# A decode kernel's GELU mixer moved from VectorE to GpSimd, with its output weights on a hardware queue in transfers of 120 and 8 partitions

## The chip, the cores and the metric

The kernel runs on one core of one Trainium2 chip. The metric is the device time in microseconds. The kernel before takes 1303.7 us (median of 4 runs, 1302.6 to 1304.4).

Engine names: PE is TensorE, DVE is VectorE, ACT is ScalarE, POOL is GpSimd, SP is SyncE. SP here only issues DMA transfers.

## The reference

One token attends to a cache of 65536 positions, with 8 KV heads of 256 (2 query heads each). Beside it runs a small mixer on the same token: a layer norm, then a sum over 1792 hidden units of GELU, for each of 448 channels. A sigmoid gate blends both.

```python
g = sigmoid((x * gate_w).sum(-1))                  # x: (1, 1, 448)
q = (x @ wq).reshape(16 heads, 256)
p = softmax(q @ k.T / 16)                          # k, v: 8 heads x 65536 x 256, bf16
a = (p @ v).reshape(4096) @ wo                     # wo: 4096 x 448
u = gelu(layernorm(x)[d] * w1[f] + b1[f])          # 448 x 1792
b = u @ w2 + b2
out = g * a + (1 - g) * b
```

K and V are 537 MB together. The output weights `wo` are only 3.67 MB, and the mixer is 14 blocks of 128 hidden units.

## The kernel before

K and V stream in chunks of 8192 positions (4 MB each) through a ring of five 32 KB slots per partition, all on SP's queue. Each chunk is worked on in four steps: transposes on PE, a copy from PSUM on DVE, scores on PE, exp on ACT, a transpose of p on DVE, and P-V on PE four steps later. The output weights of KV head g (512 rows, 448 KB) come on GpSimd's queue, two heads ahead. These are the parts that the change and the argument touch:

```python
def load_wo(g):                                   # GpSimd's (software) queue, 128 partitions
    nc.gpsimd.dma_start(
        out=wo_t[g % 2][:],
        in_=A_wo[g * 512:(g + 1) * 512, :].rearrange("(q p) n -> p q n", p=128),
    )
# ...
def mixer_open(b):
    nc.scalar.activation(out=t_b, in_=h_bc, func=ACT.Square, scale=w1T[:, b], bias=b1T[:, b])
    nc.vector.tensor_scalar(out=u_b, in0=h_bc, ...)            # u = h*w1 + b1
def mixer_mid(b):
    nc.vector.tensor_scalar(out=t_b, in0=t_b, ...)             # C1*u^2 + 1
    nc.vector.tensor_tensor(out=t_b, in0=t_b, in1=u_b, op=ALU.mult)
    nc.scalar.activation(out=t_b, in_=t_b, func=ACT.Tanh, scale=GELU_C0)
def mixer_close(b):
    nc.vector.scalar_tensor_tensor(out=gel, in0=t_b, scalar=1.0, in1=u_b, ...)
    nc.tensor.matmul(y_ps, lhsT=w2T[:, b:b + 1], rhs=gel, ...)
# ... one block every two steps, so the mixer is over after 30 of the 256 steps
for n in range(n_steps + LAG):
    transposes(n, 0); scores(n - 1); transposes(n, 1); p_transpose(n - 1)
    mixer(n)
    epilogue(n)
    p_v(n - LAG)
    # a load of the ring slot that has just come free, on SP
```

The softmax here doesn't subtract the row's maximum and nothing guards it: scores larger than these inputs give would overflow.

Of the kernel before, what the change touches and what calls it, by code (L numbers as in the profile page):

```python
# [8 lines left out]
FP32 = mybir.dt.float32  # L9
# [7 lines left out]
DH = 256  # L17


NB = 64  # L20
# [14 lines left out]
def kernel(  # L35
# [46 lines left out]
    LAST_K = [SB] * STEPS  # L82
    LAST_V = [2 * SB, SB, SB // 2 + 2, SB // 2 - 2]

    def load(item):
        i, is_v = divmod(item, 2)
        g, c = divmod(i, n_chunks)
        src = (A_v_cache if is_v else A_k_cache)[0, g, c * CHUNK:(c + 1) * CHUNK, :]
        src = src.rearrange("(p j) d -> p (j d)", j=NB)
        dst = ring[item % RING]  # L90
        parts = [NB]
        if i == total - 1:
            parts = LAST_V if is_v else LAST_K
        j = 0
        for n in parts:
            nc.sync.dma_start(out=dst[:, j * DH:(j + n) * DH], in_=src[:, j * DH:(j + n) * DH])
            j += n
# [8 lines left out]
    for hh in range(2):  # L106
        nc.sync.dma_start(
            out=wqb[64 * hh:64 * hh + 64, :], in_=A_wq[DA:D, 8 * DH * hh:8 * DH * (hh + 1)]
        )
# [4 lines left out]
    xa = const.tile([128, KA], BF16)  # L114
    xb = const.tile([128, 2], BF16)
    gwa = const.tile([128, KA], BF16)
    gwb = const.tile([128, 1], BF16)
    nc.vector.memset(xb[:], 0.0)
    nc.vector.memset(gwb[:], 0.0)
    x_row = A_x[0, 0]  # L120
    nc.scalar.dma_start(out=xa[:], in_=x_row[0:DA].rearrange("(p k) -> p k", k=KA))
    for hh in range(2):
        nc.scalar.dma_start(
            out=xb[64 * hh:64 * hh + 64, hh:hh + 1], in_=x_row[DA:D].rearrange("(p o) -> p o", o=1)
        )
    nc.gpsimd.dma_start(out=gwa[:], in_=gate_w[0:DA].rearrange("(p k) -> p k", k=KA))
    nc.gpsimd.dma_start(out=gwb[0:64, :], in_=gate_w[DA:D].rearrange("(p o) -> p o", o=1))

    xB = work.tile([128, D], FP32, name="xB")
    nc.gpsimd.dma_start(out=xB[:], in_=x_row.partition_broadcast(128))  # L130
# [11 lines left out]
    def load_wo(g):  # L142
        nc.gpsimd.dma_start(
            out=wo_t[g % 2][:],
            in_=A_wo[g * 512:(g + 1) * 512, :].rearrange("(q p) n -> p q n", p=128),
        )
# [4 lines left out]
    ones_f = const.tile([128, 128], FP32)  # L151
    nc.gpsimd.memset(ones_f[:], 1.0)


    sel = const.tile([128, 2, 2], FP32)
    same = const.tile([128, 4, 32], FP32)
    nc.gpsimd.memset(sel[:], 0.0)
    nc.gpsimd.memset(same[:], 0.0)
    for a in range(4):
        nc.gpsimd.affine_select(  # L160
            out=sel[:].rearrange("p h r -> p (h r)"), in_=sel[:].rearrange("p h r -> p (h r)"),
            compare_op=ALU.not_equal, fill=1.0, base=-32 * a, pattern=[[-1, 4]],
            channel_multiplier=1,
        )
        for half in range(16):
            nc.gpsimd.affine_select(
                out=same[:, :, 2 * half:2 * half + 2], in_=same[:, :, 2 * half:2 * half + 2],
                compare_op=ALU.not_equal, fill=1.0, base=-32 * a, pattern=[[0, 4], [-16, 2]],
                channel_multiplier=1,
            )  # L170

# [8 lines left out]
    acc = work.tile([1, D], FP32, name="acc")  # L180
    res = work.tile([1, D], BF16, name="res")
# [4 lines left out]
    nc.vector.memset(pv[:], 0.0)  # L186


    xg = const.tile([128, KA + 1], FP32)
    nc.vector.tensor_tensor(out=xg[:, 0:KA], in0=xa[:], in1=gwa[:], op=ALU.mult)  # L190
    nc.vector.tensor_tensor(out=xg[:, KA:KA + 1], in0=xb[:, 0:1], in1=gwb[:], op=ALU.mult)
    xg1 = const.tile([128, 1], FP32)
    nc.vector.tensor_reduce(out=xg1[:], in_=xg[:], axis=AXIS.X, op=ALU.add)
    z_ps = misc[:, 500:501]
    nc.tensor.matmul(z_ps, lhsT=ones_f[:], rhs=xg1[:], start=True, stop=True)
# [5 lines left out]

    stats = const.tile([128, nc.vector.BN_STATS_DIM], FP32)
    nc.vector.bn_stats(out=stats[:], in_=xB[:])
# [4 lines left out]
    mhalf = const.tile([128, 1], FP32)  # L208
    nc.gpsimd.memset(mhalf[:], -0.5)
# [3 lines left out]
    for _ in range(2):  # L213
# [6 lines left out]
    h_bc = xB  # L220
    nc.vector.tensor_scalar(
        out=h_bc[:], in0=xB[:], scalar1=mv[:, 0:1], scalar2=rstd[:, 0:1],
# [7 lines left out]
    for c in range(2):  # L230
        for h in range(HQ):
            dst = q_ps[:, c * HQ + h:c * HQ + h + 1]
            for k in range(KA):
                nc.tensor.matmul(
                    dst, lhsT=wqa_v[:, k, h, :, c], rhs=xa[:, k:k + 1], start=(k == 0), stop=False
                )
            nc.tensor.matmul(
                dst, lhsT=wqb_v[:, h % 8, :, c], rhs=xb[:, h // 8:h // 8 + 1],
                start=False, stop=True,
            )  # L240
# [10 lines left out]
    y_ps = misc[0:1, 0:D]  # L251
    u_b = work.tile([128, D], FP32, name="u_b")
    t_b = work.tile([128, D], FP32, name="t_b")
    gel = work.tile([128, D], BF16, name="gel")

    def mixer_open(b):
        nc.scalar.activation(
            out=t_b[:], in_=h_bc[:], func=ACT.Square, scale=w1T[:, b:b + 1], bias=b1T[:, b:b + 1]
        )
        nc.vector.tensor_scalar(  # L260
            out=u_b[:], in0=h_bc[:], scalar1=w1T[:, b:b + 1], scalar2=b1T[:, b:b + 1],
            op0=ALU.mult, op1=ALU.add,
        )

    def mixer_mid(b):
        nc.vector.tensor_scalar(
            out=t_b[:], in0=t_b[:], scalar1=GELU_C1, scalar2=1.0, op0=ALU.mult, op1=ALU.add
        )
        nc.vector.tensor_tensor(out=t_b[:], in0=t_b[:], in1=u_b[:], op=ALU.mult)  # L269
        nc.scalar.activation(out=t_b[:], in_=t_b[:], func=ACT.Tanh, scale=GELU_C0)  # L270

    def mixer_close(b):
        nc.vector.scalar_tensor_tensor(  # L273
            out=gel[:], in0=t_b[:], scalar=1.0, in1=u_b[:], op0=ALU.add, op1=ALU.mult
        )
        nc.tensor.matmul(
            y_ps, lhsT=w2T[:, b:b + 1], rhs=gel[:], start=(b == 0), stop=(b == NF - 1)
        )

    def mixer_end():  # L280
        nc.vector.tensor_scalar(
            out=acc[:], in0=y_ps, scalar1=0.5, scalar2=b2[0:1, 0:1], op0=ALU.mult, op1=ALU.add
        )
        nc.vector.tensor_scalar(
            out=acc[:], in0=acc[:], scalar1=gate[0:1, 1:2], scalar2=None, op0=ALU.mult
        )

    mix_pitch = max(1, min(2, (steps_g + LAG - 2) // (NF + 1)))

    def mixer(n):  # L290
        if mix_pitch == 1:
            if n < NF:
                mixer_open(n)
                mixer_mid(n)
                mixer_close(n)
            if n == NF:
                mixer_end()
            return
        b, ph = divmod(n - 2, 2)
        if ph == 0:  # L300
            if 0 < b <= NF:
                mixer_close(b - 1)
            if b == NF:
                mixer_end()
# [159 lines left out]
```

## Time and profile before

| | before |
|---|---|
| time, median | 1303.7 us |
| bytes moved | 545.7 MB, mean 419 GB/s |
| stream when nothing holds it up | 430 to 433 GB/s |
| PE, DVE busy | 74%, 62% |
| mean granted clock of TensorE | 0.85 |

This is the page's strip of 40 equal slices (32.6 us each; digits are busy tenths), and the DMA queues (packets, MB, share of the time of 16 engines):

```profile
DVE  2666668655655756656656656646556646657557
...
POOL 5000000000000000000000000000000000000000
...
DMA  9998889999999999999999999999999999999995
GB/s 358 428 421 377 370 354 383 430 432 429 430 432 431 432 433 433 431 432 431 431 433 429 432 432 430 432 430 434 431 432 432 430 433 432 432 433 431 429 429 251
...
q1 hardware_dynamic: 19602, 540.55, 96.9%
q0 software_dynamic: 1584, 3.92, 0.8%
q8 instruction: 66, 1.08, 0.3%
```

The stream runs at its full rate from slice 7 on (this text counts slices from 0, the prediction from 1). It falls to 354 to 383 GB/s in slices 3 to 6, while the strip of DVE has nothing unusual. The table of windows says it in fixed stretches; its last three columns are the granted clock (of TensorE, as a share of full speed), the share of the DMA engines that is busy, and GB/s:

```profile
core 0: us, PE busy (x) PEld busy (x) DVE busy (x) ACT busy (x) POOL busy (x), PEclk, DMA share, GB/s
40.00:50.00 10.00, 2.52 (x16) 1.71 (x16) 2.75 (x5) 0.58 (x1) 0.00 (x0) 0.56 1.00 419
100.00:120.00 20.00, 16.87 (x129) 10.07 (x129) 12.21 (x17) 4.02 (x9) 0.00 (x0) 0.76 0.86 353
160.00:180.00 20.00, 15.26 (x119) 9.39 (x118) 13.76 (x17) 4.44 (x11) 0.00 (x0) 0.81 0.81 335
200.00:220.00 20.00, 16.87 (x159) 10.33 (x159) 16.82 (x21) 3.90 (x11) 0.00 (x0) 0.91 0.83 342
240.00:260.00 20.00, 14.88 (x128) 9.20 (x128) 11.41 (x12) 2.75 (x8) 0.00 (x0) 0.83 1.00 428
```

Between 80 and 220 us the DMA engines are idle up to a fifth of the time. The list of waits tells why (us in total, times, the longest):

```profile
engine line waited for: us in total, times, longest us
...
PE tps_74 L316 <- DMA ring_71<-in_A_k_cache_dram: 66.3, 12, 8.4
...
PE misc L276 <- DVE gel L273: 43.1, 14, 3.1
...
ACT t_b L257 <- DVE gel L273: 30.8, 13, 3.2
```

In each of 14 blocks PE waits 3.1 us for the mixer's last DVE operation, because on DVE that operation stands behind big copies of 1.2 us each (in the timeline at 62 us: two copies and a transpose). The ring slots come free late, and the stream runs dry. Added up over the seven 20-us windows from 80 to 220 us, the shortfall against 431.5 GB/s is 19 us of streaming.

The end of the timeline (start, duration, engine, line, operation):

```profile
1296.91 0.60 PE L348 MATMUL pv<-ring_71,pT_332 128*4 128x512 bf16 x8
...
1298.38 1.05 PE L374 MATMUL misc<-sel,pvs 128*128 128x2 f32 x8 [0.86 <-DVE pvs L365]
...
1299.68 0.92 PE L384 MATMUL misc<-wo_109,oT 128*1 128x448 bf16 x4 [0.26 <-DVE oT L378]
...
1301.28 0.32 SPq L433 DMA_DIRECT2D out_dram<-res  x1
```

The last P-V starts at 1296.91, when the last piece of V is there; from then on the close takes 6.6 us. In this part PE and the stream end together.

### The profile page before, as it was taken

Reading aid. Unit: us, or ns where it says so; the run is one execution under the profiler, and the core shown is the slowest. Engines: PE = TensorE matmul, PEld = TensorE weight load, DVE = VectorE, ACT = ScalarE, POOL = GpSimd, SP = SyncE. Lnnn points to the kernel's source line nnn. Section 1 sums busy time; section 2 is a strip of 40 time slices with the busy share of each in tenths; the row PEclk is TensorE's granted clock in tenths of the full one; section 3 lists DMA queues with packets and bytes.
Section 4 is the critical chain, followed back from the end, with each engine's and each line's share of the span. In section 5 each row is a group of like instructions: output and inputs, shape, how many; then the busy total and the mean of one; then the engine's idle time right before and its main releaser. Section 6 shows DMA issues by size and latency. Waiting matters only on the chain.

```text
span 1303.5 us, 19519 instructions
## 1 busy us (share of the span) xinstructions
PE 962.2 (74%) x8448; PEld 600.4 (46%) x8448; DVE 810.3 (62%) x897; ACT 194.7 (15%) x543; POOL 22.7 (2%) x94
## 2 busy tenths in 40 slices
PE   3577778776777876867876876867877867868778
PEld 2344445444444444544544544544544544445444
DVE  2666668655655756656656656646556646657557
ACT  0122221111111111111111111111111111111111
POOL 5000000000000000000000000000000000000000
PEclk9777789888978878888888888889888878888889
DMA  9998889999999999999999999999999999999995
GB/s 358 428 421 377 370 354 383 430 432 429 430 432 431 432 433 433 431 432 431 431 433 429 432 432 430 432 430 434 431 432 432 430 433 432 432 433 431 429 429 251
DMA packets 21575, 545.71 MB, mean 419 GB/s; under 512 B 3057, under 2 KB 3314, under 8 KB 4466
## 3 DMA queue, kind: packets, MB, share of 16 engines
q1 hardware_dynamic: 19602, 540.55, 96.9%
q0 software_dynamic: 1584, 3.92, 0.8%
q8 instruction: 66, 1.08, 0.3%
q14 instruction: 19, 0.16, 0.0%
q10 hardware_dynamic: 304, 0.00, 0.0%
HBM read 544.34 MB, written 0.00 MB: 418 GB/s over the span
## 4 chain that ended last, share of the span: by engine, by line
DMA 54%; PE 38%; DVE 7%; issue 1%; ACT 0%; ACTq 0%
PE tps_74 L316 13%; PE tps_75 L316 12%; DMA ring_71<-in_A_k_cache_dram 12%; DMA ring_73<-in_A_k_cache_dram 12%; DMA ring_69<-in_A_k_cache_dram 11%; DMA ring_70<-in_A_k_cache_dram 10%; DMA ring_72<-in_A_k_cache_dram 9%; PE pv L348 6%; PE sc_77 L326 3%; PE sc_76 L326 3%; DVE kT_325 L317 2%; DVE kT_326 L317 1%; DMA xa<-in_A_x_dram 1%; DVE t_b L269 1%; DVE gel L273 1%
## 5 line engine op out<-in xcount | busy, mean ns | idle before, releaser
L317 DVE COPY kT_325<-tps_74 128x2048 bf16<-128x2048 bf16 x128 | 154.8, 1209 | 302.2 <-PE tps_74 L316 302.2
L317 DVE COPY kT_325<-tps_75 128x2048 bf16<-128x2048 bf16 x128 | 156.6, 1224 | 85.6 <-PE tps_75 L316 85.0
L317 DVE COPY kT_326<-tps_74 128x2048 bf16<-128x2048 bf16 x128 | 153.2, 1197 | 43.8 <-PE tps_74 L316 42.8
L317 DVE COPY kT_326<-tps_75 128x2048 bf16<-128x2048 bf16 x128 | 156.8, 1225 | 36.3 <-PE tps_75 L316 36.2
L332 ACT ACTIVATE p_328<-sc_77 128x512 bf16<-128x512 f32 x128 | 76.2, 595 | 620.5 <-PE sc_77 L326 620.5
L332 ACT ACTIVATE p_327<-sc_76 128x512 bf16<-128x512 f32 x128 | 76.4, 597 | 385.4 <-PE sc_76 L326 385.4
L316 PE MATMUL tps_74<-ident,ring_71 128*128 128x128 f32 x416 | 69.8, 322 | 66.3 <-DMA ring_71<-in_A_k_cache_dram 66.3
L316 PE MATMUL tps_74<-ident,ring_69 128*128 128x128 f32 x416 | 67.8, 316 | 58.5 <-DMA ring_69<-in_A_k_cache_dram 58.5
L316 PE MATMUL tps_74<-ident,ring_73 128*128 128x128 f32 x416 | 69.2, 320 | 53.3 <-DMA ring_73<-in_A_k_cache_dram 53.3
L326 PE MATMUL sc_77<-kT_326,qT 128*32 128x512 bf16 x1024 | 101.6, 481 | 1.2 <-DVE kT_326 L317 1.2
L316 PE MATMUL tps_74<-ident,ring_70 128*128 128x128 f32 x416 | 67.0, 313 | 48.0 <-DMA ring_70<-in_A_k_cache_dram 48.0
L316 PE MATMUL tps_74<-ident,ring_72 128*128 128x128 f32 x384 | 63.6, 319 | 49.0 <-DMA ring_72<-in_A_k_cache_dram 49.0
L316 PEld LDWEIGHTS tps_74<-ident,ring_71 128*128 128x128 f32 x416 | 55.5, 165 | 92.1 <-issue 92.1
L316 PEld LDWEIGHTS tps_74<-ident,ring_69 128*128 128x128 f32 x416 | 54.0, 161 | 81.4 <-issue 72.3
L316 PEld LDWEIGHTS tps_74<-ident,ring_73 128*128 128x128 f32 x416 | 54.8, 163 | 78.5 <-issue 77.6
L316 PEld LDWEIGHTS tps_74<-ident,ring_70 128*128 128x128 f32 x416 | 53.1, 160 | 72.6 <-issue 72.2
L316 PEld LDWEIGHTS tps_74<-ident,ring_72 128*128 128x128 f32 x384 | 50.5, 164 | 72.5 <-issue 70.4
L326 PE MATMUL sc_76<-kT_325,qT 128*32 128x512 bf16 x1024 | 83.2, 402 | 0.2
L316 PE MATMUL tps_75<-ident,ring_71 128*128 128x128 f32 x416 | 65.1, 306 | 0.0
L316 PE MATMUL tps_75<-ident,ring_73 128*128 128x128 f32 x416 | 64.7, 306 | 0.0
L316 PEld LDWEIGHTS tps_75<-ident,ring_73 128*128 128x128 f32 x416 | 51.7, 157 | 28.0 <-issue 28.0
L316 PEld LDWEIGHTS tps_75<-ident,ring_71 128*128 128x128 f32 x416 | 51.6, 157 | 27.9 <-issue 27.9
(125 smaller groups left out, 951.6 us busy)
## 6 DMA issues: line engine op xcount, KB each, us to landing
ring_69<-in_A_k_cache_dram SPq DMA_DIRECT2D x13, 4096.0 KB, 24.0
ring_70<-in_A_v_cache_dram SPq DMA_DIRECT2D x13, 4096.0 KB, 33.2
ring_71<-in_A_k_cache_dram SPq DMA_DIRECT2D x13, 4096.0 KB, 24.1
ring_72<-in_A_v_cache_dram SPq DMA_DIRECT2D x13, 4096.0 KB, 33.7
ring_73<-in_A_k_cache_dram SPq DMA_DIRECT2D x13, 4096.0 KB, 25.0
ring_69<-in_A_v_cache_dram SPq DMA_DIRECT2D x13, 4096.0 KB, 33.6
ring_70<-in_A_k_cache_dram SPq DMA_DIRECT2D x12, 4096.0 KB, 24.4
ring_71<-in_A_v_cache_dram SPq DMA_DIRECT2D x12, 4096.0 KB, 33.5
```

Of the source, the lines that this page charges most:

```text
L269: nc.vector.tensor_tensor(out=t_b[:], in0=t_b[:], in1=u_b[:], op=ALU.mult)
L273: nc.vector.scalar_tensor_tensor(out=gel[:], in0=t_b[:], scalar=1.0, in1=u_b[:], op0=ALU.add, op1=ALU.mult)
L316: nc.tensor.transpose(tp[:, 128 * jj:128 * jj + 128], kn[:, j0 + jj, :], ident[:])
L317: nc.vector.tensor_copy(out=kT[n % 2][:, 8 * DH * half:8 * DH * (half + 1)], in_=tp[:].bitcast(BF16))
L326: nc.tensor.matmul(sc[n % 2][32 * a:32 * a + 32, :], lhsT=qT[:, c, g].rearrange("p r x -> p (r x)"), rhs=kv[:, :, 32 * a:32 * a + 32, c], ...
L332: nc.scalar.activation(out=p_t[n % 2][:], in_=sc[n % 2][:], func=ACT.Exp, scale=scale, accum_out=den[g % 2][:, n % steps_g:n % steps_g + 1],)
L348: nc.tensor.matmul(pv[32 * a:32 * a + 4, :], lhsT=pT[:, i, :, 0], rhs=vt[:, j * DH:(j + 2) * DH], start=first and i < 4, stop=last and i > ...
```

## The change

The intent: take the mixer off VectorE, which feeds PE; give the weight loads to a hardware queue on few DMA engines; make the start cheaper (x as a row, few tiny transfers); and let the last chunk of V arrive interleaved with K. In the diff, cut to its core, the mixer is spread over eight steps a block, so it lasts until about step 116.

```diff
     def load_wo(g):
-        nc.gpsimd.dma_start(
-            out=wo_t[g % 2][:],
-            in_=A_wo[g * 512:(g + 1) * 512, :].rearrange("(q p) n -> p q n", p=128),
-        )
+        src = A_wo[g * 512:(g + 1) * 512, :].rearrange("(q p) n -> p q n", p=128)
+        for lo, hi in ((0, 120), (120, 128)):
+            nc.scalar.dma_start(out=wo_t[g % 2][lo:hi, :, :], in_=src[lo:hi, :, :])
@@ mixer: one block per MIX = 8 steps
-            nc.vector.tensor_scalar(out=u_b, in0=h_bc, ...)
+            nc.gpsimd.tensor_scalar(out=u_b, in0=h_bc, ...)
+            nc.gpsimd.tensor_scalar(out=t_b, in0=t_b, ...)
+            nc.gpsimd.tensor_tensor(out=t_b, in0=t_b, in1=u_b, op=ALU.mult)
+        if ph == 2:
+            nc.scalar.activation(out=t_b, in_=t_b, func=ACT.Tanh, scale=GELU_C0)
+            nc.gpsimd.tensor_scalar(out=t_b, in0=t_b, scalar1=1.0, ...)
+            nc.gpsimd.tensor_tensor(out=gel, in0=t_b, in1=u_b, op=ALU.mult)
+        if ph == 5:
+            nc.tensor.matmul(misc[0:1, 0:D], lhsT=w2T[:, b:b + 1], rhs=gel, start=True, stop=True)
+            nc.vector.scalar_tensor_tensor(out=acc, in0=misc[0:1, 0:D], ...)   # one partition
@@ start: new small tiles in the pool that lies ahead of the ring
-    xa, xb, gwa, gwb: x and gate_w spread over partitions; xB: x broadcast to 128 partitions
+    x_row = const.tile([1, D], BF16); gw_row = const.tile([1, D], BF16)
+    # ... x is turned by five matmuls, and broadcast by one
@@ last chunk
+    (k, 0, SB), (k, SB, SB), (k, 2 * SB, SB), (v, 0, SB), (k, 3 * SB, SB), (v, SB, SB), ...
```

More of the change, by code (lines that the diff above doesn't have):

```diff
@@ L81, with piece @@
     total = HKV * n_chunks
-    LAST_K = [SB] * STEPS
-    LAST_V = [2 * SB, SB, SB // 2 + 2, SB // 2 - 2]
-    def load(item):
+    def piece(item, j, n):
         i, is_v = divmod(item, 2)
@@ L89, in load @@
         src = src.rearrange("(p j) d -> p (j d)", j=NB)
-        dst = ring[item % RING]
-        parts = [NB]
-        if i == total - 1:
-            parts = LAST_V if is_v else LAST_K
-        j = 0
-        for n in parts:
-            nc.sync.dma_start(out=dst[:, j * DH:(j + n) * DH], in_=src[:, j * DH:(j + n) * DH])
-            j += n
+        nc.sync.dma_start(
+            out=ring[item % RING][:, j * DH:(j + n) * DH], in_=src[:, j * DH:(j + n) * DH]
+        )
+    def load(item):
+        if item < 2 * total - 2:
+            piece(item, 0, NB)
+        elif item == 2 * total - 1:
+            k, v = item - 1, item
+            tail = SB // 2 - 2
+            for it, j, n in (
+                (k, 0, SB), (k, SB, SB), (k, 2 * SB, SB), (v, 0, SB), (k, 3 * SB, SB),
+                (v, SB, SB), (v, 2 * SB, SB), (v, 3 * SB, SB - tail), (v, NB - tail, tail),
+            ):
+                piece(it, j, n)
     wq_slot = ring[RING - 1]
@@ L105 @@
     )
-    for hh in range(2):
-        nc.sync.dma_start(
-            out=wqb[64 * hh:64 * hh + 64, :], in_=A_wq[DA:D, 8 * DH * hh:8 * DH * (hh + 1)]
-        )
+    nc.sync.dma_start(out=wqb, in_=A_wq[DA:D, :].rearrange("r (hh n) -> (r hh) n", hh=2))
     for item in range(RING - 1):
         load(item)
-    xa = const.tile([128, KA], BF16)
-    xb = const.tile([128, 2], BF16)
-    gwa = const.tile([128, KA], BF16)
-    gwb = const.tile([128, 1], BF16)
-    nc.vector.memset(xb[:], 0.0)
-    nc.vector.memset(gwb[:], 0.0)
-    x_row = A_x[0, 0]
-    nc.scalar.dma_start(out=xa[:], in_=x_row[0:DA].rearrange("(p k) -> p k", k=KA))
-    for hh in range(2):
-        nc.scalar.dma_start(
-            out=xb[64 * hh:64 * hh + 64, hh:hh + 1], in_=x_row[DA:D].rearrange("(p o) -> p o", o=1)
-        )
-    nc.gpsimd.dma_start(out=gwa[:], in_=gate_w[0:DA].rearrange("(p k) -> p k", k=KA))
-    nc.gpsimd.dma_start(out=gwb[0:64, :], in_=gate_w[DA:D].rearrange("(p o) -> p o", o=1))
-    xB = work.tile([128, D], FP32, name="xB")
-    nc.gpsimd.dma_start(out=xB[:], in_=x_row.partition_broadcast(128))
+    x_row = const.tile([1, D], BF16)
+    nc.scalar.dma_start(out=x_row[:], in_=A_x[0])
+    gw_row = const.tile([1, D], BF16)
+    nc.scalar.dma_start(out=gw_row[:], in_=gate_w.rearrange("(o n) -> o n", o=1))
     w1T = const.tile([128, NF], FP32)
@@ L142, in load_wo @@
     def load_wo(g):
-        nc.gpsimd.dma_start(
-            out=wo_t[g % 2][:],
-            in_=A_wo[g * 512:(g + 1) * 512, :].rearrange("(q p) n -> p q n", p=128),
-        )
+        src = A_wo[g * 512:(g + 1) * 512, :].rearrange("(q p) n -> p q n", p=128)
+        for lo, hi in ((0, 120), (120, 128)):
+            nc.scalar.dma_start(out=wo_t[g % 2][lo:hi, :, :], in_=src[lo:hi, :, :])
     ident = const.tile([128, 128], FP32)
     make_identity(nc, ident[:])
-    ones_f = const.tile([128, 128], FP32)
-    nc.gpsimd.memset(ones_f[:], 1.0)
-    sel = const.tile([128, 2, 2], FP32)
-    same = const.tile([128, 4, 32], FP32)
+    sel = const.tile([128, 4], FP32)
+    pick = const.tile([128, 2], FP32)
+    same = const.tile([128, 64, 2], FP32)
     nc.gpsimd.memset(sel[:], 0.0)
-    nc.gpsimd.memset(same[:], 0.0)
-    for a in range(4):
-        nc.gpsimd.affine_select(
-            out=sel[:].rearrange("p h r -> p (h r)"), in_=sel[:].rearrange("p h r -> p (h r)"),
-            compare_op=ALU.not_equal, fill=1.0, base=-32 * a, pattern=[[-1, 4]],
-            channel_multiplier=1,
-        )
-        for half in range(16):
+    nc.gpsimd.memset(pick[:], 0.0)
+    for t, w, step in ((sel, 4, -1), (pick, 2, -16)):
+        for a in range(4):
             nc.gpsimd.affine_select(
-                out=same[:, :, 2 * half:2 * half + 2], in_=same[:, :, 2 * half:2 * half + 2],
-                compare_op=ALU.not_equal, fill=1.0, base=-32 * a, pattern=[[0, 4], [-16, 2]],
-                channel_multiplier=1,
-            )
+                out=t[:], in_=t[:], compare_op=ALU.not_equal, fill=1.0, base=-32 * a,
+                pattern=[[step, w]], channel_multiplier=1,
+            )
+    nc.gpsimd.tensor_copy(
+        out=same[:], in_=pick[:].rearrange("p (o r) -> p o r", o=1).to_broadcast([128, 64, 2])
+    )
+    mhalf = const.tile([128, 1], FP32)
+    nc.gpsimd.memset(mhalf[:], -0.5)
+    one_b = const.tile([1, 128], BF16)
+    nc.vector.memset(one_b[:], 1.0)
+    one_f = const.tile([1, 128], FP32)
+    nc.vector.memset(one_f[:], 1.0)
     kT = [work.tile([128, SB * DH], BF16, name=f"kT{i}") for i in range(2)]
@@ L180 @@
     acc = work.tile([1, D], FP32, name="acc")
+    half_g = work.tile([1, 1], FP32, name="half_g")
     res = work.tile([1, D], BF16, name="res")
@@ L186 @@
     nc.vector.memset(pv[:], 0.0)
-    xg = const.tile([128, KA + 1], FP32)
-    nc.vector.tensor_tensor(out=xg[:, 0:KA], in0=xa[:], in1=gwa[:], op=ALU.mult)
-    nc.vector.tensor_tensor(out=xg[:, KA:KA + 1], in0=xb[:, 0:1], in1=gwb[:], op=ALU.mult)
-    xg1 = const.tile([128, 1], FP32)
-    nc.vector.tensor_reduce(out=xg1[:], in_=xg[:], axis=AXIS.X, op=ALU.add)
+    nc.vector.memset(acc[:], 0.0)
+    xd = const.tile([1, 2, 128], BF16)
+    nc.vector.memset(xd[:], 0.0)
+    for hh in range(2):
+        nc.vector.tensor_copy(
+            out=xd[:, hh, :].rearrange("o (r two) -> o r two", two=2)[:, :, hh],
+            in_=x_row[:, DA:D],
+        )
+    x_ps = misc[:, 480:480 + KA + 2]
+    for k in range(KA + 2):
+        if k < KA:
+            row = x_row[:, 0:DA].rearrange("o (p k) -> o p k", k=KA)[:, :, k]
+        else:
+            row = xd[:, k - KA, :]
+        nc.tensor.matmul(x_ps[:, k:k + 1], lhsT=row, rhs=one_b[:, 0:1], start=True, stop=True)
+    xT = const.tile([128, KA + 2], BF16)
+    nc.vector.tensor_copy(out=xT[:], in_=x_ps)
+    u_b = work.tile([128, D], FP32, name="u_b")
+    xg = u_b[0:1, :]
+    nc.vector.tensor_tensor(out=xg, in0=x_row[:], in1=gw_row[:], op=ALU.mult)
+    z1 = const.tile([1, 1], FP32)
+    nc.vector.tensor_reduce(out=z1[:], in_=xg, axis=AXIS.X, op=ALU.add)
     z_ps = misc[:, 500:501]
-    nc.tensor.matmul(z_ps, lhsT=ones_f[:], rhs=xg1[:], start=True, stop=True)
+    nc.tensor.matmul(z_ps, lhsT=one_f[:], rhs=z1[:], start=True, stop=True)
     nc.scalar.activation(out=gate[:, 0:1], in_=z_ps, func=ACT.Exp, scale=-1.0)
@@ L199 @@
     nc.vector.reciprocal(out=gate[:], in_=gate[:])
+    xb_ps = sc[0][:, 0:D]
+    nc.tensor.matmul(xb_ps, lhsT=one_b[:], rhs=x_row[:], start=True, stop=True)
     stats = const.tile([128, nc.vector.BN_STATS_DIM], FP32)
-    nc.vector.bn_stats(out=stats[:], in_=xB[:])
+    nc.vector.bn_stats(out=stats[:], in_=xb_ps)
     mv = const.tile([128, nc.vector.BN_AGGR_DIM], FP32)
@@ L207 @@
     nc.vector.tensor_scalar(out=veps[:], in0=mv[:, 1:2], scalar1=1e-5, scalar2=None, op0=ALU.add)
-    mhalf = const.tile([128, 1], FP32)
-    nc.gpsimd.memset(mhalf[:], -0.5)
     rstd = const.tile([128, 1], FP32)
@@ L219 @@
         nc.vector.tensor_tensor(out=rstd[:], in0=rstd[:], in1=nt[:], op=ALU.mult)
-    h_bc = xB
+    h_bc = work.tile([128, D], FP32, name="h_bc")
     nc.vector.tensor_scalar(
-        out=h_bc[:], in0=xB[:], scalar1=mv[:, 0:1], scalar2=rstd[:, 0:1],
+        out=h_bc[:], in0=xb_ps, scalar1=mv[:, 0:1], scalar2=rstd[:, 0:1],
         op0=ALU.subtract, op1=ALU.mult,
@@ L234 @@
                 nc.tensor.matmul(
-                    dst, lhsT=wqa_v[:, k, h, :, c], rhs=xa[:, k:k + 1], start=(k == 0), stop=False
+                    dst, lhsT=wqa_v[:, k, h, :, c], rhs=xT[:, k:k + 1], start=(k == 0), stop=False
                 )
+            x_h = KA + h // 8
             nc.tensor.matmul(
-                dst, lhsT=wqb_v[:, h % 8, :, c], rhs=xb[:, h // 8:h // 8 + 1],
-                start=False, stop=True,
+                dst, lhsT=wqb_v[:, h % 8, :, c], rhs=xT[:, x_h:x_h + 1], start=False, stop=True
             )
@@ L248 @@
     load_wo(1)
-    y_ps = misc[0:1, 0:D]
-    u_b = work.tile([128, D], FP32, name="u_b")
     t_b = work.tile([128, D], FP32, name="t_b")
     gel = work.tile([128, D], BF16, name="gel")
-    def mixer_open(b):
-        nc.scalar.activation(
-            out=t_b[:], in_=h_bc[:], func=ACT.Square, scale=w1T[:, b:b + 1], bias=b1T[:, b:b + 1]
-        )
-        nc.vector.tensor_scalar(
-            out=u_b[:], in0=h_bc[:], scalar1=w1T[:, b:b + 1], scalar2=b1T[:, b:b + 1],
-            op0=ALU.mult, op1=ALU.add,
-        )
@@ L265, in mixer_mid @@
-    def mixer_mid(b):
-        nc.vector.tensor_scalar(
-            out=t_b[:], in0=t_b[:], scalar1=GELU_C1, scalar2=1.0, op0=ALU.mult, op1=ALU.add
-        )
-        nc.vector.tensor_tensor(out=t_b[:], in0=t_b[:], in1=u_b[:], op=ALU.mult)
-        nc.scalar.activation(out=t_b[:], in_=t_b[:], func=ACT.Tanh, scale=GELU_C0)
-    def mixer_close(b):
-        nc.vector.scalar_tensor_tensor(
-            out=gel[:], in0=t_b[:], scalar=1.0, in1=u_b[:], op0=ALU.add, op1=ALU.mult
-        )
-        nc.tensor.matmul(
-            y_ps, lhsT=w2T[:, b:b + 1], rhs=gel[:], start=(b == 0), stop=(b == NF - 1)
-        )
@@ L280, in mixer_end @@
-    def mixer_end():
-        nc.vector.tensor_scalar(
-            out=acc[:], in0=y_ps, scalar1=0.5, scalar2=b2[0:1, 0:1], op0=ALU.mult, op1=ALU.add
-        )
-        nc.vector.tensor_scalar(
-            out=acc[:], in0=acc[:], scalar1=gate[0:1, 1:2], scalar2=None, op0=ALU.mult
-        )
-    mix_pitch = max(1, min(2, (steps_g + LAG - 2) // (NF + 1)))
-    def mixer(n):
-        if mix_pitch == 1:
-            if n < NF:
-                mixer_open(n)
-                mixer_mid(n)
-                mixer_close(n)
-            if n == NF:
-                mixer_end()
+    MIX = min(8, (n_steps - LAG) // (NF + 1))
@@ L298, in mixer @@
+    def mixer(n):
+        b, ph = divmod(n - LAG, MIX)
+        if not 0 <= b < NF:
             return
-        b, ph = divmod(n - 2, 2)
         if ph == 0:
-            if 0 < b <= NF:
-                mixer_close(b - 1)
-            if b == NF:
-                mixer_end()
-            if 0 <= b < NF:
-                mixer_open(b)
-        elif 0 <= b < NF:
-            mixer_mid(b)
+            nc.scalar.activation(
+                out=t_b[:], in_=h_bc[:], func=ACT.Square, scale=w1T[:, b:b + 1],
+                bias=b1T[:, b:b + 1],
+            )
+            nc.gpsimd.tensor_scalar(
+                out=u_b[:], in0=h_bc[:], scalar1=w1T[:, b:b + 1], scalar2=b1T[:, b:b + 1],
+                op0=ALU.mult, op1=ALU.add,
+            )
+            nc.gpsimd.tensor_scalar(
+                out=t_b[:], in0=t_b[:], scalar1=GELU_C1, scalar2=1.0, op0=ALU.mult, op1=ALU.add
+            )
+            nc.gpsimd.tensor_tensor(out=t_b[:], in0=t_b[:], in1=u_b[:], op=ALU.mult)
+        if ph == 2:
+            nc.scalar.activation(out=t_b[:], in_=t_b[:], func=ACT.Tanh, scale=GELU_C0)
+            nc.gpsimd.tensor_scalar(
+                out=t_b[:], in0=t_b[:], scalar1=1.0, scalar2=None, op0=ALU.add
+            )
+            nc.gpsimd.tensor_tensor(out=gel[:], in0=t_b[:], in1=u_b[:], op=ALU.mult)
+        if ph == 5:
+            nc.tensor.matmul(
+                misc[0:1, 0:D], lhsT=w2T[:, b:b + 1], rhs=gel[:], start=True, stop=True
+            )
+            if b == 0:
+                nc.vector.tensor_scalar(
+                    out=half_g[:], in0=gate[0:1, 1:2], scalar1=0.5, scalar2=None, op0=ALU.mult
+                )
+                nc.vector.tensor_scalar(
+                    out=acc[:], in0=acc[:], scalar1=b2[0:1, 0:1], scalar2=gate[0:1, 1:2],
+                    op0=ALU.add, op1=ALU.mult,
+                )
+            nc.vector.scalar_tensor_tensor(
+                out=acc[:], in0=misc[0:1, 0:D], scalar=half_g[0:1, 0:1], in1=acc[:],
+                op0=ALU.mult, op1=ALU.add,
+            )
@@ L358, in den_tot @@
         nc.tensor.matmul(
-            d_ps, lhsT=same[:].rearrange("p a m -> p (a m)"), rhs=dsum[:], start=True, stop=True
+            d_ps, lhsT=same[:].rearrange("p o r -> p (o r)"), rhs=dsum[:], start=True, stop=True
         )
@@ L374, in o_turn @@
                 nc.tensor.matmul(
-                    o_ps[:, 2 * c:2 * c + 2], lhsT=pvs[:, lo:lo + 128], rhs=sel[:, half, :],
+                    o_ps[:, 2 * c:2 * c + 2], lhsT=pvs[:, lo:lo + 128], rhs=sel[:, 2 * half:2 * half + 2],
                     start=(half == 0), stop=(half == 1),
```

## The prediction

> **What bounds it now.** The cache stream. The page shows 16 DMA engines always busy at 430 to 433 GB/s from 240 us on. A chunk of K and V (8.39 MB) arrives in 19.4 us; in the chain of waits its four steps take PE and DVE about 14 us, then PE waits for the next K. Three places fall short of 431.5 GB/s:
> - 80 to 220 us (table of windows: 417, 353, 394, 392, 335, 374, 342 GB/s per 20 us): 19 us of stream lost, where the mixer runs on VectorE. In the timeline a block of two steps takes 11.5 us against 9.7 for the stream: 2.1 us of DVE work, and PE waits 3.1 us at the mixer's matmul for DVE's `gel`, 14 times (list of waits: 43 us). Ring slots come free late and the DMA engines run dry.
> - The first 20 us: 305 and 336 GB/s[...].
> - The end: the last V pieces (3 KB packets) finish on eight engines at about 1285.5 us, on the other eight at 1293 to 1297 us. The late ones appear to be those that also carry the instruction fetches (66 packets of 16 KB, durations repeating with period eight). The last P-V starts at 1296.9; the close after it takes 6.6 us.
>
> **What changes.**
> 1. Mixer to GpSimd, one block per eight steps. [...] Five fit in eight steps (39 us); Tanh has two steps for the first three, so ACT hardly waits. Gain: 18.5 of the 19 us.
> 2. Output weights (8 x 448 KB). Now packets of 4480 B at 177 ns: about 9 us on each of 16 engines. Rows of 896 B I estimate at 43 ns (packets of 3, 5 and 8 KB give about 9 ns + 37 ns/KB): 64 rows an engine and load, 22 us on each of eight engines. If these are the early eight: early 1285.5 - 18.5 - 9 + 22 = 1280, late 1296.9 - 18.5 - 9 = 1269, so the end moves to 1280. If the late eight, 1291. [...] Chances 50, 25 and 25%.
> 3. Start: no 2-byte packets, no 128-row broadcast, no 64 selects on POOL; but the q projection still waits for its weights (landing near 16 us). Gain about 1 us.
> 4. Last chunk: K3 lands 2.4 us later, but PE, at 3.13 us a step, needs it only 23 us after the previous K. V has the same last piece: about 0.
>
> **Predicted.** 1280 + 6.6 - 1 = 1286 us; 8 in 10: 1278 to 1297. Faster by over 2%: 0.08; within 2%: 0.91; slower by over 2%: 0.01.
>
> **What would show it.** (1) About 430 GB/s in slices 4 to 7, no wait for DVE at the mixer's matmul, POOL busy to about 590 us. (2) 896 B packets in ScalarE's queue; finishing times closer together or reversed; completion packets tell 8 engines or 15. (3) Slices 1 and 2 higher. (4) The close still 6 to 7 us.
>
> **What would make it wrong.** GpSimd operations over 3 us,[...] so that ACT waits in Tanh and holds back the exp; rows over 43 ns; the loaded engines being the late ones.

Four passages that no trace or run had shown are cut from this text: the size of GpSimd's operations with where it came from ("Five fit in eight steps" means the five of them in a block; after the change they took 4.9 of the 39 us); "or blocked by DVE"; the cause given for the slow first 20 us; and the third case for the weights, 120 partitions on 15 engines, which put the end at about 1281 us and had the last of the three chances, 25%. The sum: 1285.5 - 18.5 - 9 + 22 = 1280, and 1280 + 6.6 - 1 = 1285.6, put as 1286 us. That the transfer would run on eight engines, on which the 22 us rest, was the assumption.

## The result

| | before | after |
|---|---|---|
| time, median | 1303.7 us | 1304.0 us (1303.7 to 1306.9) |
| ratio | | 1.0008, 95% interval 0.9991 to 1.0025 |

The time is the same. A ratio here is the mean time of one kernel's fast runs over that of the other's of the same rounds, so it is not quite the ratio of the medians that are quoted. The profiled run of after was its slowest (1306.9 us).

The same lines of the page after:

```profile
DVE  3556755656656567566566465674665655656657
...
POOL 1100111101111001110000000000000000000000
...
DMA  9999999999999999999999999999999999999995
GB/s 393 374 432 431 430 428 427 413 431 429 432 422 412 433 429 430 422 414 431 432 428 416 421 431 429 429 406 421 432 430 430 402 421 431 429 430 415 433 426 213
...
q1 hardware_dynamic: 19730, 540.55, 97.5%
q10 hardware_dynamic: 4284, 3.67, 0.9%
q8 instruction: 66, 1.08, 0.3%
```

The dip in slices 3 to 6 is gone, as predicted. In its place there is a dip in slice 1, and then in every place where weights are loaded: 413, 412, 414, 416, 406 and 402 GB/s, about every fifth slice from slice 7 on. The weights are now in q10: 4284 packets, of which 4096 are weight pieces of 896 B.

```profile
core 0: us, PE busy (x) PEld busy (x) DVE busy (x) ACT busy (x) POOL busy (x), PEclk, DMA share, GB/s
40.00:50.00 10.00, 4.12 (x24) 2.94 (x24) 1.23 (x1) 1.15 (x3) 0.00 (x0) 0.52 0.79 246
100.00:120.00 20.00, 15.24 (x130) 9.27 (x129) 12.09 (x14) 3.10 (x9) 3.20 (x3) 0.83 0.99 424
160.00:180.00 20.00, 15.44 (x134) 9.33 (x136) 12.44 (x13) 3.87 (x10) 3.07 (x4) 0.83 1.01 433
200.00:220.00 20.00, 14.29 (x129) 9.26 (x132) 12.07 (x15) 3.18 (x8) 3.04 (x3) 0.83 1.00 427
240.00:260.00 20.00, 13.40 (x128) 8.24 (x126) 11.53 (x13) 3.69 (x10) 3.17 (x4) 0.83 1.00 411
```

From 80 to 220 us the stream runs at 424 to 437 GB/s. The window from 240 to 260 us, beside which both kernels load weights, went from 428 to 411, and 40 to 50 us from 419 to 246.

```profile
engine line waited for: us in total, times, longest us
...
PE tps_74 L316 <- DMA ring_71<-in_A_k_cache_dram: 73.5, 13, 9.1
...
PEld L293 <- issue: 2.3, 14, 0.2
```

PE still waits for K, and a little longer than before (73.5 us for this slot instead of 66.3): that is the stream setting the pace. The wait for `gel` is gone from the mixer's matmul (now L293); only 2.3 us of issue time is left there. GpSimd's five operations take 0.57 to 1.33 us each, 4.9 us for a block (busy us, mean ns of one, idle before):

```profile
L288 POOL TENSOR_SCALAR t_b<-t_b 128x448 f32<-128x448 f32 x14 | 18.6, 1332 | 73.1 <-ACT t_b L287 73.1
L291 POOL TENSOR_TENSOR gel<-t_b,u_b 128x448 bf16<-128x448 f32 x14 | 16.0, 1141 | 1.2
L285 POOL TENSOR_TENSOR t_b<-t_b,u_b 128x448 f32<-128x448 f32 x14 | 16.0, 1140 | 1.2
L278 POOL TENSOR_SCALAR u_b<-h_bc,w1T,b1T 128x448 f32<-128x448 f32 x14 | 10.1, 719 | 6.7 <-DVE qT L256 5.3
L282 POOL TENSOR_SCALAR t_b<-t_b 128x448 f32<-128x448 f32 x14 | 7.9, 568 | 419.4 <-ACT t_b L274 419.4
```

The list of SP's waits has a new kind, K and V loads that wait for weight loads:

```profile
SPq L88 <- DMA wo_98<-in_A_wo_dram: 96.5, 7, 34.3
SPq L88 <- DMA wo_99<-in_A_wo_dram: 66.1, 7, 21.9
```

The packed records of the issues explain it: in after all loads on the two hardware queues raise the same eight completion semaphores in turn (numbers 107, 109, 110 and 114 to 118; the landings are recorded on these eight). The second V load waits for semaphore 114 and then uses it itself. The first weight transfer of 120 partitions, issued at 8.74 us, had used 114 before it; its last landing is at 45.94 us, and the V load goes out at 45.96, almost 35 us after the load ahead of it (start, duration):

```profile
11.21 0.43 SPq L88 DMA_DIRECT2D ring_71<-in_A_k_cache_dram  x1
45.96 0.33 SPq L88 DMA_DIRECT2D ring_72<-in_A_v_cache_dram  x1
```

The end of the timeline:

```profile
1297.06 0.60 PE L348 MATMUL pv<-ring_71,pT_148 128*4 128x512 bf16 x8
...
1298.53 1.63 PE L374 MATMUL misc<-sel,pvs 128*128 128x2 f32 x8 [0.86 <-DVE pvs L365]
...
1300.41 1.65 PE L384 MATMUL misc<-wo_99,oT 128*1 128x448 bf16 x4 [0.25 <-DVE oT L378]
...
1302.73 0.32 SPq L433 DMA_DIRECT2D out_dram<-res  x1
```

So the gain that I predicted was there, and something took all of it back. The theory at this point (A): the weight loads, by their small pieces and by the held-up load at the start. The rival (B): the loads are innocent, and the gain is lost in the tail or to GpSimd.

### The profile page after: what moved, and what is told of

Read it like the earlier page. It is cut to its first block, busy times and chain, and to the rows that moved or that the text cites. A ratio compares the mean times of both kernels' runs of the same rounds, so it can differ in the third digit from the quotient of the medians.

```text
span 1305.1 us, 19519 instructions
## 1 busy us (share of the span) xinstructions
PE 958.5 (73%) x8454; PEld 601.4 (46%) x8454; DVE 792.2 (61%) x859; ACT 193.3 (15%) x543; POOL 74.2 (6%) x93
## 3 DMA queue, kind: packets, MB, share of 16 engines
q10 hardware_dynamic: 4284, 3.67, 0.9%
## 4 chain that ended last, share of the span: by engine, by line
DMA 63%; PE 36%; DVE 1%; issue 0%; ACTq 0%; ACT 0%; SPq 0%; DVEq 0%
DMA ring_73<-in_A_k_cache_dram 13%; PE tps_74 L316 12%; DMA ring_69<-in_A_k_cache_dram 12%; DMA ring_72<-in_A_k_cache_dram 12%; DMA ring_70<-in_A_k_cache_dram 11%; DMA ring_71<-in_A_k_cache_dram 11%; PE tps_75 L316 11%; PE pv L348 5%; PE sc_77 L326 4%; DMA wo_98<-in_A_wo_dram 3%; PE sc_76 L326 3%; DMA gw_row<-in_gate_w_dram 0%; PE misc L293 0%; DVE kT_142 L317 0%; PE misc L384 0%
## 5 line engine op out<-in xcount | busy, mean ns | idle before, releaser
L317 DVE COPY kT_142<-tps_75 128x2048 bf16<-128x2048 bf16 x128 | 156.8, 1225 | 25.1 <-PE tps_75 L316 24.5
L316 PE MATMUL tps_74<-ident,ring_71 128*128 128x128 f32 x416 | 68.5, 318 | 73.5 <-DMA ring_71<-in_A_k_cache_dram 73.5
```

The source lines that it names most:

```text
L316: nc.tensor.transpose(tp[:, 128 * jj:128 * jj + 128], kn[:, j0 + jj, :], ident[:])
L317: nc.vector.tensor_copy(out=kT[n % 2][:, 8 * DH * half:8 * DH * (half + 1)], in_=tp[:].bitcast(BF16))
```

## The experiments

Every experiment ran in rounds with the kernel before on the same chip. "Ratio" is to before. Two numbers are worked out from the records of the DMA transfers in the traces, in which each entry is a packet; one of 32 KB is a partition's share of a chunk of K or V. They are the mean duration of the 32 KB K and V packets while weights are on the way (loads three to eight), and in a quiet stretch without any (about 610 to 670 us of the span). The last column is the mean of the 66 packets of 16 KB that fetch instructions.

| run | median us | ratio | 32 KB during a load, ns | 32 KB quiet, ns | fetch, ns |
|---|---|---|---|---|---|
| before | 1303.7 | 1 | 1228 | 1215.7 | 961 |
| after | 1304.0 | 1.0008 | 1274 | 1218.5 | 1075 |
| a_sw | 1290.0 | 0.9887 | 1253 | 1217.9 | 1069 |
| b_hw | 1317.2 | 1.0099 | 1262 | 1214.9 | 981 |
| a_hw128 | 1292.8 | 0.9911 | 1224 | 1218.4 | 1065 |
| a_late | 1305.6 | 1.0010 | 1272 | 1218.9 | 1071 |
| a_112 | 1302.5 | 0.9977 | 1269 | 1218.5 | 1074 |
| a_64 | 1308.4 | 1.0023 | 1300 | 1218.5 | 1068 |
| a_big | 1305.1 | 0.9999 | 1324 | 1218.2 | 1072 |
| b_mix | 1286.7 | 0.9856 | 1228 | 1214.8 | 959 |
| a_sw_pad | 1283.7 | 0.9846 | 1229 | 1215.5 | 957 |
| a_pad | 1299.0 | 0.9965 | 1273 | 1214.8 | 980 |
| m_low | 1293.3 | 0.9919 | 1302 | 1218.6 | 1068 |
| m_mid | 1283.7 | 0.9845 | 1225 | 1219.3 | 1068 |
| b_off | 1312.1 | 1.0062 | 1248 | 1220.3 | 1066 |
| b_128 | 1312.2 | 1.0061 | 1250 | 1218.6 | 1061 |
| a_sw_pad32 | 1289.6 | 0.9894 | 1252 | 1218.6 | 1070 |
| a_sw_pad_last | 1284.0 | 0.9847 | 1228 | 1215.5 | 960 |
| a_hw128_pad_late | 1284.8 | 0.9853 | 1216 | 1215.5 | 953 |

The 95% intervals of the ratios are about 0.0015 to 0.0022 to either side. Names with a_ and m_ start from the changed kernel, names with b_ from the one before.

### First set: is it the weight loads?

**a_sw**: the weights back on GpSimd's queue.

```diff
-        for lo, hi in ((0, 120), (120, 128)):
-            nc.scalar.dma_start(out=wo_t[g % 2][lo:hi, :, :], in_=src[lo:hi, :, :])
+        nc.gpsimd.dma_start(out=wo_t[g % 2][:], in_=src)
```

> The changed kernel with the output weights back on GpSimd's queue, one transfer of 128 partitions; mixer, start and last chunk stay changed. Theory A (the mixer's move gains about 19 us, and the hardware-queue weight loads give it back through 896 B rows and a held-up load at the start): 1285 to 1289 us, slice 1 back to about 430 GB/s, about 429 GB/s in the slices with a weight load. Theory B (the loads are innocent; the gain is lost in the tail or to GpSimd's work): 1300 us or more.

Measured: 1290.0 us, and no dips at the loads:

```profile
GB/s 391 432 430 430 429 432 425 432 430 431 431 426 432 430 431 429 427 431 430 431 429 427 430 430 431 429 429 428 430 433 430 426 429 433 427 432 422 428 428 215
```

The loads cost about 14 us, so B falls. But 1290 is above the range of A: something else is missing too.

**b_hw**: the other way round, the kernel before with the change's `load_wo`.

> The kernel before with only the output weights moved to ScalarE's hardware queue in transfers of 120 and 8 partitions. Theory A: 10 to 16 us slower than before (six later loads at 1.7 us each and the start), 1313 to 1319 us, less if the first loads hide in the mixer's stretch. Theory B: within 3 us of before.

Measured: 1317.2 us, 12.7 us slower. It is the weight loads in either kernel.

**a_hw128**: one transfer of 128 partitions on ACT's queue.

```diff
-        for lo, hi in ((0, 120), (120, 128)):
+        for lo, hi in ((0, 128),):
```

> The changed kernel with each weight load as one hardware-queue transfer of 128 partitions, so on 16 engines instead of 15 and 8. Theory A (cost lies in the number of 896 B rows, 512 a load whatever the split): 1301 to 1305 us, the same 412 to 421 GB/s in the slices with a load. Rival C (the uneven split over 15 and 8 engines is what costs): 1285 to 1292 us.

Measured: 1292.8 us, with the same 4096 pieces of 896 B:

```profile
GB/s 397 428 376 437 430 429 428 430 432 428 431 431 427 430 429 432 427 431 426 433 430 427 430 431 430 430 430 427 430 432 431 426 429 433 428 431 428 425 426 241
```

This refutes A's number of small pieces. The dips at the later loads are gone (from slice 3 to 35 nothing is under 426 GB/s), the 32 KB packets beside them take 1224 ns instead of 1274, and most of the loss is gone. Only a dip in slice 2 is left, from a V load that waits 36 us for a weight load. It is the split into 120 and 8 that costs: either that it is uneven (rival C), or something else about it.

**a_late**: the first two weight loads at steps 10 and 20.

```diff
-    load_wo(0)
-    load_wo(1)
+        if n in (10, 20):          # after epilogue(n), in the loop
+            load_wo(n // 10 - 1)
```

> The changed kernel with the first two weight loads issued at steps 10 and 20 of the loop instead of before it. Theory A: the second V load no longer waits for a weight load, slice 1 goes from 374 to about 415 to 430 GB/s, 3 to 5 us faster than the changed kernel, about 1300 us. If the stall at the start is made up later anyway: 1303 to 1305 us.

Measured: 1305.6 us; no gain, a miss. The dip in slice 1 is gone (432 GB/s), but slices 2 to 5 fall to 411 to 424, where the two loads now run. The held-up V load at the start is plain to see, but moving the loads away from it gained nothing. This run can't price the hold-up alone, because the two loads now run beside the full stream instead (its packets beside a load take 1272 ns in this run). With one transfer of 128 partitions the late issue seems to be worth some 2 us: an estimate from a_hw128 and a_hw128_pad_late (below), less the address effect (ratios 0.9911 - 0.0041 - 0.9853), no more than its uncertainty.

### Second set: what about the split?

How many engines a transfer uses I read from its completion packets of 4 B. On SP's queue in after there are 2193 = 137 x 16 + 1: 16 for each of 137 loads of 128 partitions, one for the single row of the output. In q10 there are 186: 2 for the two one-row loads, and 184 = 8 x 23 for the weights. The landings on the semaphores split the 23: apart from one record soon after the issue (mostly 0.5 us), each transfer of 120 partitions has 15 and each of 8 has 8. The records do not name a packet's engine. I take one completion packet for one of the 16 engines of the page, so that the 120 partitions run on 15 engines, not on eight. The single transfer of a_hw128 leaves 130 = 2 + 8 x 16.

That left the question which partitions an engine writes. Theory D was my conjecture: a piece that is written by another engine than the one which writes K and V to that partition takes time from both. I call such partitions foreign, and the assignment of partitions to engines the map. The map that I used was an assumption; no run shows it.

**a_112**: 112 and 16 partitions. Both use 16 engines, evenly (258 completion packets = 2 + 8 x 32).

```diff
-        for lo, hi in ((0, 120), (120, 128)):
+        for lo, hi in ((0, 112), (112, 128)):
```

> The changed kernel with weight transfers of 112 and 16 partitions: two per load as in the change, but both on 16 engines with 32 rows each. Theory D (a row written by another engine than the one whose share of a 128-partition transfer holds that partition takes time from both engines[...]): [...]1301 to 1306 us and 32 KB packets of about 1262 ns during a load. Rival C (the uneven split over 15 and 8 engines costs): as the single transfer, 1290 to 1294 us, packets of 1224 ns. Rival E (two transfers instead of one on the shared eight completion semaphores): 1301 to 1306 us with packets of 1224 ns.

Measured: 1302.5 us and 1269 ns. An even split over 16 engines costs nearly as much as the uneven one, so C falls. E falls by the packets' durations (and by m_low below, where a single transfer stretches them to 1302 ns).

**a_64**: `((0, 64), (64, 128))`.

> The changed kernel with weight transfers of 64 and 64 partitions: two per load, 16 engines, 32 rows each. Theory D: [...]1296 to 1300 us, 32 KB packets of about 1243 ns during a load. Rival C: 1290 to 1294 us. Rival E: 1301 to 1306 us.

Measured: 1308.4 us and 1300 ns: the slowest of the kernels that start from the changed one, where D had 1296 to 1300 us and 1243 ns. So D, as I counted it, fails here. Why 64 and 64 is the slowest split was not shown.

**a_big**: the same 120 and 8, but with a partition's two rows adjacent in memory: 1792 B pieces, half as many.

```diff
-        src = A_wo[...].rearrange("(q p) n -> p q n", p=128)
+        src = A_wo[...].rearrange("(r p c) n -> p r (c n)", p=128, c=2)
@@ o_turn
-                lo = half * DH + c * 128
+                lo = half * DH + c
-                    ..., lhsT=pvs[:, lo:lo + 128], ...
+                    ..., lhsT=pvs[:, lo:lo + 255:2], ...
```

> The changed kernel (120 and 8 partitions) with another order of the weight rows, so that a partition's two rows are adjacent in memory: 1792 B pieces, half as many, same bytes, correct result. If the loss of theory D goes with the bytes written to a foreign share: 1300 to 1304 us. If it goes with the number of pieces: 1294 to 1298 us.

Measured: 1305.1 us. A 32 KB packet beside a piece is longer by 106 ns over its quiet time (1324 - 1218), against 56 ns (1274 - 1218.5) for half the bytes. So the loss goes with bytes, not with pieces.

**b_mix**: the kernel before with the mixer of the change, nothing else.

> The kernel before with only the mixer moved to GpSimd, one block per eight steps (start, weights and last chunk as before). If the mixer's move carries the gain of the changed kernel with software-queue weights: 1287 to 1293 us, about 430 GB/s in slices 3 to 6. If the new start or the last chunk carries it: 1297 us or more.

Measured: 1286.7 us, ratio 0.9856, so 18.8 us faster (slices 3 to 6 at 427 to 437 GB/s). And this kernel, which keeps the old start and the old last chunk, beats a_sw by 3 us (4 by the ratios). Its quiet packets take 1214.8 ns, where all kernels with the new start have about 1218, and its instruction fetches 959 instead of 1069. So with the new start the quiet K and V packets are about 3 ns longer. Looking for what it could touch, I compared the addresses of the tiles: the small tiles of the start lie ahead of the ring in each partition, and they had moved it from byte 26880 to byte 29344. The first is a multiple of 256, the second only of 32 (theory F).

### Third set: the address, and a shift of the partitions

**a_sw_pad**: a_sw with an unused tile of 96 B ahead of the ring, which then starts at 29440 (a multiple of 256).

```diff
     nt = const.tile([128, 1], FP32)
+    const.tile([128, 24], FP32, name="pad")
```

> The changed kernel with software-queue weights plus a 96-byte unused tile, so that the ring buffers start at a multiple of 64 B in a partition again (29440 instead of 29344; before: 26880). Theory F (the new small tiles moved the ring off a 64 B boundary and each 32 KB packet is 0.3% longer for it): quiet 32 KB packets back from 1218 to about 1215 ns, instruction fetches from 1069 to about 960 ns, 1285 to 1288 us. If the address doesn't matter: 1289 to 1291 us and 1218 ns.

Measured: 1283.7 us; packets and fetches are back to 1215.5 and 957 ns, and no slice from 1 to 35 is under 427 GB/s:

```profile
GB/s 393 433 428 433 432 430 433 431 433 430 435 427 434 430 433 432 431 429 432 434 430 431 432 432 432 433 430 432 433 432 433 428 432 434 431 433 421 435 427 243
```

**a_pad**: the changed kernel with the same tile.

> The changed kernel itself plus the same 96-byte pad. Theory F: 3 to 5 us faster than the changed kernel, 1299 to 1301 us; 32 KB packets during a weight load still about 1260 ns if their stretching comes from which engine writes which partition, about 1225 ns if it came from the address.

Measured: 1299.0 us, 5 us better than the change. The packets beside a load keep their 1273 ns, so with 120 and 8 partitions the stretch does not come from the address. With the software queue part of it does: 35 ns over quiet in a_sw, 14 in a_sw_pad.

**m_low and m_mid**: one transfer of 64 partitions per load, of partitions 0 to 63 or 32 to 95, on 16 engines (130 completion packets both, so 16 a load). Half of the weights stay zero, so the computation is wrong on purpose. (The comparison with the reference still passed: with these inputs the attention's share of the output is within its tolerance.)

```diff
+    for t in wo_t:
+        nc.gpsimd.memset(t[:], 0.0)
-        for lo, hi in ((0, 120), (120, 128)):
+        for lo, hi in ((0, 64),):      # m_low;  ((32, 96),) in m_mid
```

> The changed kernel with only 64 partitions of each weight load, 0 to 63, in one transfer on 16 engines; the rest of the tile stays zero, so the result is wrong on purpose. [...] Theory D: 32 KB packets of 1270 to 1310 ns during a load, as with 64 and 64 partitions, and 5 to 9 us slower than the run with partitions 32 to 95.

> As the run with partitions 0 to 63, but partitions 32 to 95 (wrong on purpose): same bytes, same count of transfers and pieces, same 16 engines[...]. Theory D: 32 KB packets of about 1225 ns during a load, 1288 to 1292 us. If the map doesn't matter: same times and packets as with partitions 0 to 63.

Measured: 1293.3 us and 1302 ns for m_low, 1283.7 us and 1225 ns for m_mid. First m_low, then m_mid:

```profile
GB/s 383 416 432 429 431 432 416 425 436 424 435 418 422 431 430 429 419 425 435 426 434 413 433 428 432 427 412 434 426 434 430 407 432 432 427 430 410 429 430 257
```

```profile
GB/s 398 430 426 431 431 431 428 429 431 431 430 428 430 431 430 432 428 431 428 431 433 426 432 428 431 432 429 429 430 432 428 429 430 432 431 429 423 431 424 234
```

Shifting one transfer by 32 partitions, with bytes, pieces and completion packets equal, is worth 9.6 us. So which partitions a transfer covers matters, in the direction that D had with my assumed map. But m_mid came out below its range of 1288 to 1292 us, and the pair does not show why the packets beside m_low's loads are longer: no record names the engine that writes a partition. Both runs move half the weights, so their times do not compare with those of the complete kernels.

### Fourth set: closing the budget

**b_off** and **b_128**: the kernel before with an unused tile of 32 or 128 B, so that its ring starts at 26912 or 27008. **a_sw_pad32**: a pad of 32 B in a_sw, the ring at 29376.

> The kernel before plus an unused 32-byte tile, so that the ring starts at 26912, 32 B past a 64 B boundary (before: 26880). Theory F: quiet 32 KB packets from 1215.7 to about 1218 ns, instruction fetches from 961 to about 1070 ns, 3 to 6 us slower than before, 1307 to 1310 us. If the address acted only together with the other changes: within 1 us of before.

> The changed kernel with software-queue weights and a pad of 32 B instead of 96: the ring at 29376, a multiple of 64 but not of 128 or 256. If the 64 B boundary is what counts: as with 96 B, 1283 to 1285 us, quiet packets about 1215 ns. If 128 or 256 B is needed: as without a pad, 1289 to 1291 us, 1218 ns.

> The kernel before plus an unused 128-byte tile: the ring at 27008, a multiple of 128 but not of 256. If 128 B is enough: within 2 us of before, quiet 32 KB packets 1215 to 1216 ns, instruction fetches about 960 ns. If 256 B is needed: as with a 32-byte shift, 1310 to 1313 us, 1218 to 1221 ns, about 1070 ns.

Measured: 1312.1 us for b_off and 1312.2 us for b_128, both about 8 us slower than before for a tile that nothing uses (b_off above its range); 1289.6 us for a_sw_pad32, as without a pad. F is right for the kernel before too, but my boundary of 64 B was wrong: multiples of 32, 64 and 128 B are slow, and the two starts that are fast (26880 and 29440) are multiples of 256. Quiet packets take about 1215 ns with these two and 1218 to 1220 with the others, and instruction fetches about 960 against 1066 ns. Why, no run shows.

**a_sw_pad_last**: a_sw_pad with the last chunk loaded as before.

> The changed kernel with software-queue weights, 96 B pad, and the last chunk loaded as in the kernel before. If the new last chunk is worth nothing, as predicted: 1283 to 1285 us, and the 3 us are the start's. If the last chunk is worth the 3 us: 1286 to 1288 us.

Measured: 1284.0 us. The new last chunk is worth nothing, as predicted.

**a_hw128_pad_late**: one transfer of 128 partitions on ACT's queue, the 96 B pad, the first two loads at steps 10 and 20.

> The changed kernel with the 96 B pad, each weight load as one hardware-queue transfer of 128 partitions, the first two issued at steps 10 and 20 of the loop. If engine map, address and held-up load are all there is: 1282 to 1285 us, slice 2 at about 430 instead of 376 GB/s, as fast as the software queue. If the hardware queue costs by itself: 1287 us or more.

Measured: 1284.8 us, and the 32 KB packets beside a load take 1216 ns, as if there were no load. The hardware queue as such costs nothing that these runs resolve. This kernel and a_sw_pad are the best; both beat before by 1.5% and the change by as much, and the difference between them is within the noise.

## Why the prediction was wrong

The budget, by ratios (times 1304 us):

| part | predicted | measured | from |
|---|---|---|---|
| mixer to GpSimd | -18.5 | -18.8 | b_mix |
| new start and last chunk, without the address effect | -1 and 0 | -1.3 | a_sw_pad against b_mix |
| (of it, last chunk) | (0) | (-0.1) | a_sw_pad against a_sw_pad_last |
| ring off a multiple of 256 B | not seen | +5.3 | a_sw against a_sw_pad |
| weight loads | +1.6 to +2.6 (or +12.6) | +15.8 | after against a_sw |
| sum | -18 | +1.0 | after: +1.0 |

Some of these compare kernels of different rounds through their ratios to before, so each is good to about 2 us. The four parts are differences along one chain of kernels (before, b_mix, a_sw_pad, a_sw, after), so that they add up is no check. A pair of the same rounds is one: a_pad is 15.3 us slower than a_sw_pad, against the +15.8.

1. *"Gain: 18.5 of the 19 us."* Right, in size and in mechanism: the dip in slices 3 to 6 and PE's wait for `gel` are gone. GpSimd's five operations took 0.57 to 1.33 us, 4.9 us of the 39 that eight steps last. The two with two inputs took 1.14 us; why the one that only adds 1.0 after Tanh took 1.33 us, and the one that multiplies and adds 0.57, was not shown.
2. *"Rows of 896 B I estimate at 43 ns ... so the end moves to 1280."* This is the step that failed. The pieces took 44 ns in the mean (41 in the median, loads three to eight), as estimated. But I counted only the time of the piece itself. With 120 and 8 partitions the K and V packets beside a load were also longer by 56 ns, and there are about as many of them (521 to 543 a load) as pieces (512). An estimate from these durations: (44 + 56) ns x 36 pieces x 8 loads = 29 us on the engines that have most pieces (32 and 4, if the pieces are spread evenly over 15 and 8 engines), against 7 x (165 + 35) ns x 8 = 11 us with the software queue (a_sw, where a piece took 165 ns and the packets beside it 35 ns more), so +18 us; measured +15.8. In the sum of the prediction, the weights moved the end by 1.6 us (1278.4 to 1280) or 2.6 us (15 engines, the case above). I gave that case, which by the completion packets came true, 25%; I did not ask what the pieces do to the packets beside them. The time of 1297 or so in the unlikely branch ("if the late eight, 1291") would have been nearer by chance, for another reason.
3. *"Gain about 1 us"* for the start: -1.3, which at 2 us of uncertainty neither shows nor refutes it. But the diff's new small tiles also moved the ring off a multiple of 256 B, which costs +5.3 us (by medians 5.0 in a_pad, 7.8 in b_off). *"Slices 1 and 2 higher"* (0 and 1 in this text's count) held for the first only, 358 to 393 GB/s; the second fell from 428 to 374, for the held-up V load, which I had not foreseen. No line of the diff says so; only the order and sizes of the tiles do.
4. *"About 0"* for the last chunk: right. *"The close still 6 to 7 us"*: 8.1 us in the profiled run (1297.06 to the end of the span), mostly because its last matmuls took 1.63 and 1.65 us instead of 1.05 and 0.92. The change to the kernel is not the reason: in a_hw128 they took 1.05 and 0.92 again. From 1298 to 1303 us the granted clock was 0.58 in this run and 0.77 in before.
5. *"Finishing times closer together or reversed"*: neither. In after, as before, the DMA engines fall into an early and a late group: the last 3 KB packets of V end at 1286.7 and 1294.5 us (before: 1287.5 and 1296.1), 8 to 9 us apart. Why they do is open, and so is whether instruction fetches cause it, as I supposed.

Open are also why the packets beside a load are longer with some sets of partitions than with others (1302 ns in m_low, 1225 in m_mid), why 64 + 64 is worse than 112 + 16, and whether the address acts through the ring alone, since a pad moves every tile behind it too.

## What to carry to other kernels

In a kernel like this one, whose 16 DMA engines are busy all the time (431 GB/s), do not price a small side transfer by its own duration alone: compare the big packets beside it with those of a quiet stretch, and give the side transfer the same partition shape as the stream; here that took the stretch from 56 ns to 6 or less. Check the byte addresses of the big stream's buffers after any change to the small tiles ahead of them; here a tile that nothing uses was worth 5 to 8 us. When a bundle of edits comes out at zero, run each part alone before believing that the parts do nothing: here were -19, +5 and +16.
